# TensorE's filler matmuls in the first stage: 512 columns with a rest of 128, instead of 128 throughout

## The chip, the core and the metric

The kernel runs on one core of a Trainium2 chip. The metric is the device time of one execution in microseconds (us). The time of a kernel is the median of several executions.

## What is computed

Two layers in one program. The first is sliding-window attention with a linear bias by distance (8 batches, 8 heads, 576 positions, 64 numbers per head); the second is a feed-forward layer with a squared ReLU on the 4608 tokens that come out of it.

```python
scores = scale * np.matmul(q, k.transpose(0, 1, 3, 2))
bias = slopes[:, None, None] * (-np.abs(rel).astype(np.float32))[None, :, :]
mask = (rel >= 0) & (rel < window)            # window = 128
scores = np.where(mask, scores + bias[None], -1000000000.0)
attn = np.exp(scores - np.max(scores, axis=-1, keepdims=True))
attn = attn / (np.sum(attn, axis=-1, keepdims=True) + 1e-09)
attn_out = np.matmul(attn, v).astype(np.float32)
...
h = x @ w_in                                  # x: 4608 x 512, w_in: 512 x 2048
r = np.maximum(h, 0.0)
g = r * r
return (g @ w_out).astype(np.float32)         # w_out: 2048 x 512
```

## The kernel before

Attention works on blocks of 128 positions. For a block, q and k are loaded and cast to bf16, turned so that the head dimension lies on the partitions, multiplied into scores on TensorE, passed through the exponential on ScalarE, masked on VectorE (or given the bias by a matmul, for the first blocks), and multiplied with v ("pv", line 676). VectorE divides by the row sums (lines 693 and 702) and the result, turned again, is a slice of xT, the input of the feed-forward layer.

The feed-forward layer goes over nine groups of 512 tokens: 16 steps "up" (w_in against xT, lines 806 and 823), ReLU on ScalarE (line 770), square on VectorE (line 779), and 16 steps "down" (g against w_out, line 850) whose sums are copied to SBUF and stored. The groups of attention blocks and of the feed-forward layer are interleaved, so that TensorE has work of the second layer while the first waits.

The order of all instructions is fixed before anything is issued. Each piece of work is a `Task` with an estimated duration on each engine that could do it, its dependencies, and the PSUM banks or other buffers (`Slot`) that it takes and gives back. `Plan.order` runs through the estimated times, picks for each engine the next task by due time and a table of corrections (`ADJ`), and returns the list that is then issued. For a TensorE task that starts before 30 us of estimated time, it also notes `gap`, the time for which TensorE is expected to stand idle ahead of it while its PSUM bank is already free.

In the first stage the blocks come in one at a time and TensorE often waits. Two things are done about this. Right at the start, `warm_up` (line 483) issues eight matmuls of 512 columns on a zeroed tile `warm`. And the tasks that turn q and k ("tp", line 513), the scores, pv, the turning of x ("xp", line 722) and the up steps of the first groups ("unit", line 806) begin with `fill(task, slot)` (line 283): if the task's gap is over 200 ns, `FILL` (0.7) of it is filled with matmuls on `warm`, at 56 ns for each 128 columns. They write into the bank that the task itself is about to overwrite, so the task's own matmuls follow in the same bank. The fillers are issued after the order is fixed; the plan does not count them.

The first block (block 0) is loaded as float32 on SyncE's and ScalarE's queues and cast by VectorE (line 304, kq<-stage), first k, then q. Its transposes on TensorE come in two tasks: tp0.0 for k and tp0.1 for q; the results are copied out by VectorE (line 304, kqf<-tp) and ScalarE (line 306). The biases of the first scores are matmuls of 512 columns (line 624), the scores themselves line 633.

Of the kernel before, what the change touches and what calls it, by code (L numbers as in the profile page):

```python
# [27 lines left out]
FILL = 0.7  # L28
# [178 lines left out]
def kernel(  # L207
    ctx: ExitStack, tc: tile.TileContext, q, k, v, moe_w_in, moe_w_out, out
):
    nc = tc.nc  # L210
# [45 lines left out]
    warm = const.tile([128, 512], BF16)  # L256
# [24 lines left out]
        return slot  # L281

    def fill(task, slot):
        for _ in range(int(task.gap * FILL / 56.0) if task.gap > 200.0 else 0):
            nc.tensor.matmul(slot.tile[:, 0:128], warm[:, 0:128], warm[:, 0:128], start=True, stop=True)  # L285

    def tile_of(slot):
        return tiles[slot.tag][slot.idx]
# [179 lines left out]
    for what, key in at_first.items():  # L468
        n = int(what[1:])
# [22 lines left out]
    def transpose_kq(m, due):  # L492
# [12 lines left out]
        for i in range(2):  # L505
            st = Slot(TP if m else "o")

            def tp(i=i, st=st):
                fill(t_tp[i], bank_of(st, "tp"))
                st.tile = st.tile.bitcast(BF16)  # L510
                src = kq[s_kq[m].idx][:, i * d_model:(i + 1) * d_model]
                for j in range(C):
                    nc.tensor.transpose(st.tile[:, j * 128:(j + 1) * 128],  # L513
                                        src[:, j * 128:(j + 1) * 128], ident)
            t_tp[i] = plan.add({"PE": 4 * mm(128)}, due - 60 + i, tp,
                               [t_ident, t_tp[0] if i else last["tp"], t_kq[m][min(i, len(t_kq[m]) - 1)]],
                               [st] if i else [st, sT], [s_kq[m]] if i else [], name=f"tp{m}.{i}")

            pieces = [(0, C // 2), (C // 2, C)] if m < N_EV else [(0, C)]
            for c0, c1 in pieces:  # L520
                def evac(i=i, st=st, c0=c0, c1=c1, e=len(evs[i])):
                    o = tile_of(sT)[:, i * C + c0:i * C + c1, 0:n]
                    if split:
                        src = st.tile[:, 0:512].rearrange("p (i g c) -> p c g i", i=4, c=C)[:, c0:c1]
                        o = o.rearrange("p c (g i) -> p c g i", i=4)
                    else:
                        src = st.tile[:, 0:512].rearrange("p (c s) -> p c s", c=C)[:, c0:c1, 0:n]
                    copy(evs[i][e], o, src)
                w = (c1 - c0) * n
                evs[i].append(plan.add({"ACT": act(w), "DVE": dve_p(w, 1 if split else 2)}, due - 58, evac,  # L530
                                       [t_tp[i]], [], [st], name=f"ev{m}.{i}.{c0}"))
# [3 lines left out]
    def job(j, kind, ms, due):  # L535
# [24 lines left out]
        for z, grps in enumerate(bursts):  # L560
            def scores(grps=grps):
                for g2 in grps:
                    for r in range(2):
                        bank(sS[2 * g2 + r], f"s{r}")
                fill(t_s[grps[0]], sS[2 * grps[0]])
                for g2 in grps:
                    for jj in range(2):
                        c = 2 * g2 + jj
                        for c0, w, part, mk, mq in pieces:
                            for r in range(2):  # L570
                                rows = slice(64 * r, 64 * r + 64)
                                nc.tensor.matmul(sS[2 * g2 + r].tile[:, jj * 256 + c0:jj * 256 + c0 + w],  # L572
                                                 tile_of(s_kqT[mk])[rows, c, :], tile_of(s_kqT[mq])[rows, C + c, 0:w],
                                                 start=True, stop=True)
            deps = [last["s"]]
            for m in set(ms) | set(before.values()):
                deps += t_kqT[m]
            t = plan.add({"PE": 190.0 + len(grps) * 2 * len(pieces) * mm(128 if n == 128 else 64)}, due - 32, scores,
                         deps, sS[2 * grps[0]:2 * grps[-1] + 2], rel if grps[-1] else [],
                         name=f"s{ms[0]}" + (f".{z}" if len(bursts) > 1 else ""))  # L580
            last["s"] = t
            for g2 in grps:
                t_s[g2] = t
# [65 lines left out]
    def values(j, kind, i, m, nb, sP, t_P, mb, due):  # L649
# [14 lines left out]
        for hf in range(2):  # L664
            sv = Slot("h" if j < N_PVH else "a")

            def pv(hf=hf, sv=sv):
                fill(t_pvs[hf], bank_of(sv, "pv"))
                for hi in range(4):
                    h = 2 * hi + hf if kind == "lone" else 4 * hf + hi  # L670
                    for w, mk in parts:
                        if kind == "lone":
                            prob = lone_P(sP)[:, lone_place(h) * 128:(lone_place(h) + 1) * 128]
                        else:
                            prob = Pt[sP.idx][:, place(h)].rearrange("p t q -> p (t q)")[:, w]
                        nc.tensor.matmul(sv.tile[0:n, hi * (D + 1):(hi + 1) * (D + 1)], prob,  # L676
                                         tile_of(s_v[mk])[:, h, 0:D + 1], start=mk == parts[0][1], stop=mk == m)
# [240 lines left out]
```

The softmax here doesn't subtract the row's maximum and nothing guards it: scores larger than these inputs give would overflow.

## Time and profile before

| | |
|---|---|
| median of 4 runs | 313.43 us (313.13 to 313.82) |
| the profiled execution | 313.96 us |
| its span, first to last instruction | 312.2 us |
| TensorE busy | 306.7 us, 98% of the span |
| VectorE, ScalarE, GpSimd busy | 165.9, 169.4 and 106.2 us |
| filler matmuls (line 285) | 40, of 128 columns each, between 5.9 and 17.4 us |
| TensorE idle from 7.64 to 20.00 us | 12.36 - 11.28 = 1.08 us |
| TensorE idle from 20 to 100 us | 0 |

How to read it: the profile is one execution. A row of a view is an instruction or a merged run of like instructions, with its start from the beginning of the span, its duration, engine (PE is TensorE's matmuls, PEld its weight loads, DVE VectorE, ACT ScalarE), line, what it writes and reads, and in brackets the idle time before it and what ended that. Matmuls are pipelined, so the duration of one (0.22 us for 128 columns) is longer than the distance at which they start; the distance is what a matmul costs in a stream.

### The profile page before, as it was taken

The numbers are of one execution on the slowest core, as the hardware profiler recorded it, in microseconds if no ns is written. First come the engines' busy times: TensorE is split into PE (matmuls) and PEld (weight loads), VectorE is DVE, ScalarE is ACT, GpSimd is POOL, SyncE is SP. The second block draws the span as 40 slices with busy tenths as digits, with TensorE's granted clock in tenths as the row PEclk, the third lists the DMA queues.
The fourth block names the chain that finished last, engine by engine and source line by source line (L and its number), as shares of the span: only waits on it lengthen the run. The fifth ranks groups of instructions, "written<-read, shape, count | busy, mean of one in ns | idle before, by whom it ended". The sixth has DMA issues, their size and how long they took to land.

```text
span 312.2 us, 7098 instructions
## 1 busy us (share of the span) xinstructions
PE 306.7 (98%) x2792; PEld 175.0 (56%) x2792; DVE 165.9 (53%) x496; ACT 169.4 (54%) x324; POOL 106.2 (34%) x132
## 2 busy tenths in 40 slices
PE   8999999999999999999999999999999999999996
PEld 4579657676686744555455554555444444444443
DVE  5665457376667546878577665777222222222211
ACT  2586345496685545864597756664443443434400
POOL 8943586446640933613647364000000000000000
PEclk9999999999999999999999999999999999999999
DMA  9999999999999999998999999931111100011122
GB/s 130 160 206 206 174 195 173 167 164 161 164 162 166 148 166 198 134 133 163 160 170 179 162 157 178 191 78 53 53 34 44 57 36 34 36 36 34 34 86 84
DMA packets 166290, 39.54 MB, mean 127 GB/s; under 512 B 156400, under 2 KB 161776, under 8 KB 166256
## 3 DMA queue, kind: packets, MB, share of 16 engines
q0 software_dynamic: 115184, 18.10, 87.3%
q1 hardware_dynamic: 50640, 20.65, 37.5%
q8 instruction: 22, 0.36, 0.5%
q10 hardware_dynamic: 432, 0.33, 0.4%
q14 instruction: 12, 0.10, 0.1%
HBM read 36.70 MB, written 9.44 MB: 148 GB/s over the span
## 4 chain that ended last, share of the span: by engine, by line
PE 96%; DVE 1%; ACT 1%; issue 0%
PE o L850 40%; PE h L823 27%; PE h L806 14%; PE pv L676 6%; PE s L572 5%; PE wm L483 1%; PE tp L513 1%; DVE x L702 1%; PE tp L285 1%; PE xp L722 1%; PE s L624 0%; PE s L633 0%; ACT kqf L306 0%; ACT P L641 0%; DVE kqf L304 0%
## 5 line engine op out<-in xcount | busy, mean ns | idle before, releaser
L850 PE MATMUL o<-w_out_sb,g 128*128 128x512 bf16 (+2 forms) x592 | 141.8, 373 | 0.0
L770 ACT ACTIVATE rt<-h 128x512 bf16<-128x512 f32 (+1 forms) x145 | 86.1, 601 | 88.8 <-PE h L823 69.9
L779 DVE TENSOR_TENSOR g<-rt 128x512 bf16<-128x512 bf16 (+1 forms) x145 | 60.3, 419 | 95.5 <-ACT rt L770 95.0
L823 PE MATMUL h<-xT,w_in_sb 128*128 128x512 bf16 x384 | 96.7, 379 | 0.4 <-issue 0.4
L850 PEld LDWEIGHTS <-g 128*128 128x128 bf16 x592 | 54.2, 98 | 56.9
L596 ACT ACTIVATE P<-s 128x512 bf16<-128x512 f32 x120 | 62.2, 607 | 12.9 <-PE s L572 12.9
L823 PEld LDWEIGHTS <-w_in_sb 128*128 128x128 bf16 x384 | 35.4, 98 | 40.4 <-DMA xT<-x 0.5
L456 POOL DMA_DIRECT2D kq<-in_k_dram x39 | 33.4, 857 | 42.2 <-DMA kqT<-kq 34.0
L806 PE MATMUL h<-xT,w_in_sb 128*128 128x128 bf16 (+1 forms) x512 | 46.0, 246 | 0.0
L604 DVE TENSOR_TENSOR P<-P,masks 128x512 bf16<-128x512 bf16 x96 | 38.6, 418 | 11.6 <-ACT P L596 9.1
L806 PEld LDWEIGHTS <-w_in_sb 128*128 128x128 bf16 x512 | 39.0, 98 | 5.2
L461 POOL DMA_DIRECT2D vt<-in_v_dram x32 | 27.2, 851 | 33.2 <-PE pv L676 29.2
L456 POOL DMA_DIRECT2D kq<-in_q_dram x39 | 33.5, 860 | 7.8 <-PE h L806 2.1
L702 DVE TENSOR_TENSOR x<-pv,rec 128x256 bf16<-128x256 f32 (+1 forms) x80 | 32.0, 417 | 0.8
L676 PEld LDWEIGHTS <-P 128*128 128x128 bf16 (+1 forms) x576 | 24.2, 101 | 11.3 <-DVE g L779 1.3
L676 PE MATMUL pv<-vt,P 128*128 128x65 bf16 (+1 forms) x448 | 22.8, 194 | 0.0
L304 DVE COPY osb<-o 128x512 f32<-128x512 f32 (+1 forms) x19 | 13.0, 685 | 17.2 <-PE o L850 13.5
L306 ACT ACTIVATE osb<-o 128x512 f32<-128x512 f32 (+1 forms) x18 | 10.4, 580 | 21.5 <-PE o L850 21.5
L572 PEld LDWEIGHTS <-kqT 64*128 64x128 bf16 x448 | 12.4, 94 | 7.6 <-issue 7.6
L693 DVE RECIPROCAL rec<-pv 128x4 f32<-128x4 f32 (+1 forms) x80 | 12.4, 171 | 6.2 <-PE pv L676 5.4
L572 PE MATMUL s<-kqT 64*128 64x128 bf16 (+1 forms) x256 | 15.6, 210 | 0.0
L572 PE MATMUL s<-kqT,kqT 64*128 64x128 bf16 (+1 forms) x192 | 11.4, 210 | 0.0
(46 smaller groups left out, 105.1 us busy)
## 6 DMA issues: line engine op xcount, KB each, us to landing
out_dram<-osb SPq DMA_DIRECT2D x28, 256.0 KB, 5.5
kq<-in_k_dram POOLq DMA_DIRECT2D x31, 128.0 KB, 7.1
kq<-in_q_dram POOLq DMA_DIRECT2D x31, 128.0 KB, 7.7
vt<-in_v_dram POOLq DMA_DIRECT2D x24, 128.0 KB, 7.4
w_out_sb<-in_moe_w_out_dram POOLq DMA_DIRECT2D x4, 512.0 KB, 16.4
out_dram<-osb SPq DMA_DIRECT2D x14, 128.0 KB, 2.3
w_in_sb<-in_moe_w_in_dram POOLq DMA_DIRECT2D x3, 512.0 KB, 11.7
vf<-in_v_dram POOLq DMA_DIRECT2D x8, 128.0 KB, 7.1
```

The source lines that it names most:

```text
L456: nc.gpsimd.dma_start(view(kq[s_kq[m].idx], i), source(src, m, split))
L461: nc.gpsimd.dma_start(tile_of(s_v[m])[0:n, :, 0:D], source(v, m))
L572: nc.tensor.matmul(sS[2 * g2 + r].tile[:, jj * 256 + c0:jj * 256 + c0 + w], tile_of(s_kqT[mk])[rows, c, :], tile_of(s_kqT[mq])[rows, C + c ...
L596: nc.scalar.activation(flat(Pt[sP.idx]), sS[i].tile.rearrange("p (j t) -> p j t", j=2)[:, :, lo:hi], AF.Exp, bias=0.0, scale=scale)
L604: nc.vector.tensor_tensor(flat(Pt[sP.idx]), flat(Pt[sP.idx]), flat(masks), op=ALU.mult)
L676: nc.tensor.matmul(sv.tile[0:n, hi * (D + 1):(hi + 1) * (D + 1)], prob, tile_of(s_v[mk])[:, h, 0:D + 1], start=mk == parts[0][1], stop=mk ...
L702: nc.vector.tensor_tensor(o, heads(sv)[0:n, :, 0:D], sr.tile[0:n, :].unsqueeze(2).to_broadcast([n, 4, D]), op=ALU.mult)
L770: nc.scalar.activation(srt.tile[:, 0:n], slot.tile[:, 0:n], AF.Relu, bias=0.0, scale=1.0)
L779: nc.vector.tensor_tensor(o, i, i, op=ALU.mult)
L806: nc.tensor.matmul(slot.tile[:, f * w:(f + 1) * w], w_in_sb[:, cc, fc * 128:(fc + 1) * 128], xT[:, cc, lo:lo + w], start=cc == 0, stop=cc ...
L823: nc.tensor.matmul(slot.tile, w_in_sb[:, cc, fc * 128:(fc + 1) * 128], xT[:, cc, g * 512:(g + 1) * 512], start=cc == 0, stop=cc == C - 1)
L850: nc.tensor.matmul(slot.tile[:, 0:hi - lo], gt[:, fc, t * 128:(t + 1) * 128], w_out_sb[:, fc, lo:hi], start=fc == 0, stop=fc == FCB - 1)
```

## The change

The number of fillers n is worked out as before. They are then issued as n // 4 matmuls of 512 columns and n % 4 of 128 columns. The stationary operand (128 columns of `warm`) is the same, the moving operand and the written columns are four times as wide in the wide ones. Everything else is unchanged, the table of corrections too.

```diff
     def fill(task, slot):
-        for _ in range(int(task.gap * FILL / 56.0) if task.gap > 200.0 else 0):
-            nc.tensor.matmul(slot.tile[:, 0:128], warm[:, 0:128], warm[:, 0:128], start=True, stop=True)
+        n = int(task.gap * FILL / 56.0) if task.gap > 200.0 else 0
+        for w in [512] * (n // 4) + [128] * (n % 4):
+            nc.tensor.matmul(slot.tile[:, 0:w], warm[:, 0:128], warm[:, 0:w], start=True, stop=True)
```

## The prediction

> **What bounds the kernel now.** I read the page's busy table first, then the stretches of the first 20 us, then the fillers one by one, and last the chain of waits through them. The page:
>
> ```profile
> PE 306.7 (98%) x2792; PEld 175.0 (56%) x2792; DVE 165.9 (53%) x496; ACT 169.4 (54%) x324; POOL 106.2 (34%) x132
> ```
>
> TensorE is busy in 306.7 of 312.2 us. By stretch (columns: the stretch, then busy time and count of PE, of the weight loads, DVE, ACT and POOL, then granted clock, DMA share and GB/s):
>
> ```profile
> 5.86:7.64 1.78, 1.78 (x24) 1.78 (x23) 1.13 (x7) 0.23 (x1) 1.78 (x3) 1.00 1.54 155
> 7.64:20.00 12.36, 11.28 (x169) 8.21 (x167) 7.98 (x30) 8.81 (x26) 10.19 (x13) 1.00 1.92 177
> 20.00:100.00 80.00, 80.00 (x943) 57.28 (x940) 48.64 (x146) 49.84 (x97) 40.91 (x48) 1.00 1.89 175
> ```
>
> From 20 to 100 us TensorE never rests, so a delay or a gain of the first 20 us is carried to the end at full size. Only in those 20 us can fillers matter. These are all of them:
>
> ```profile
> L285 PE MATMUL tp<-warm x26: 219/219/314, 5.9 to 12.4; 128*128 128x128 bf16 x26
> L285 PE MATMUL xp<-warm x9: 219/219/229, 11.3 to 17.4; 128*128 128x128 bf16 x9
> L285 PE MATMUL pv<-warm x5: 219/219/219, 10.2 to 10.4; 128*128 128x128 bf16 x5
> ```
>
> That is 40 fillers. The timeline shows them in five groups, each just ahead of the task that asked for it: 22 at 5.86, 5 at 10.20, 4 at 11.26, 4 at 12.20 and 5 at 17.19. The chain of waits over 4 to 10 us tells which group is on the path:
>
> ```profile
> 4.79 0.43 PE tp L513 x4
> 5.21 0.85 PE s L624 x2
> 6.07 1.73 PE tp L285 x22
> 7.79 0.24 PE tp L513 x4
> 8.03 0.02 issue
> 8.05 0.44 DVE kqf L304
> 8.49 0.02 issue
> 8.51 0.39 ACT kqf L306
> ```
>
> The group of 22 is itself a link (1.73 us), followed by the transposes of block 0's q (line 513), their evacuation by DVE and ACT, and the first scores. What that group was to cover is DVE's cast of q, and the cast is done early:
>
> ```profile
> 6.00 0.89 DVE L304 CAST kq<-stage 128x512 bf16<-128x512 f32 x1 [0.33 <-DMA stage<-in_q_dram]
> ```
>
> It ends at 6.89, yet the first transpose starts at 7.63, behind the last filler. The fillers overrun their wait by about 0.7 us. The reason is in the spacing of the single rows: fillers start 0.107 us apart from 5.86 to 6.93, and 0.056 us apart from 7.07 on. The eight warm-up matmuls of 512 columns before them start 0.427 us apart, the 512-column matmuls of line 850 after 20 us 0.216 us apart. So TensorE runs at half speed until about 7.02 us and at full speed after it, though the granted-clock column reads 1.00 throughout; half the fill ran at the slow rate.
>
> **The change part by part.** No plan input changes: the fills are issued after the plan is made, no cost in it mentions them, so order, rings and DMA issues stay as they are. A group of n narrow fillers becomes n//4 of 512 columns and n%4 of 128, the same columns exactly: 22 gives 5 and 2, each 5 gives 1 and 1, each 4 gives 1. In sum 40 matmuls with 40 weight loads become 9 wide and 4 narrow with 13 loads; 27 of each go.
>
> *The group of 22.* At half speed, four narrow take 4 x 0.1067 = 0.427 and one wide takes 0.427: no difference. At full speed, four narrow take 4 x 0.0559 = 0.2236 (22 rows from 7.073 to 8.245, fillers and transposes alike) and one wide 0.2158 (line 850): 7.8 ns less. Before the switch 11 of the 22 have run, which is 2 wide ones and most of the third; the third ends then, two wide and two narrow follow at full speed. Only two wide ones save: about 16 ns. The transposes then start at 7.615 instead of 7.631. Their own wait, the cast, has long ended, so nothing takes this back, and the next on the chain, DVE's copy, follows them.
>
> *The five at 10.20.* The pv behind them starts 0.063 after the last filler where 0.056 is the spacing: it waits for ScalarE's exponentials (one ends at 10.430). 8 ns less filling becomes 8 ns more waiting: 0. *The four at 11.26*: they end at about 11.48, the transposes behind them wait until 11.649 for DVE's normalisation (ends 11.591): 0. *The four at 12.20*: the transposes start at once and would gain 8 ns, but end at 12.65 and their evacuation waits for DVE, which is busy until 13.05: 0. *The five at 17.19*: they end at 17.48 and the transposes wait until 17.858 for DVE: 0. If that cover were gone, each group would give 8 ns, 32 ns in all.
>
> *The 27 weight loads.* Matmuls of 128 columns run 0.056 apart with a load each, and the wide ones of line 850 also have one each; the loads lie beside the matmuls. 0. The trace shows no case where a load in this stage holds back a filler.
>
> *Waits.* A wide filler writes all 512 columns of its bank, a narrow one 128. Could it wait for a reader of the rest? Only the group at 12.20 waits at all, 0.221 after the row before it, and DVE's last reading of a pv bank ends at 12.138; it reads 256 columns in one instruction, so the narrow filler waits for all of it already. The others start on the spacing of the row before them or, at 17.19, on the 0.148 that also follows other score rows. Bounds: nothing below, 0.46 us above (the idle ahead of the transposes at 13.11, which would hide it). I take 0.
>
> Sum: 313.96 (the profiled execution; its span is 312.19 and 1.77 lies around it) - 0.016 = 313.94. The median of the four runs is 313.43, 0.53 below the profiled one; the same step gives **313.4 us**.
>
> What a page says against this: the Trainium skill, "TensorE: Matmul & The Clock Gate", section "Back-to-back issue gap", has a sustained spacing of about 81 ns for 128 columns and 131 ns for 512 in streams of load and matmul. By that estimate the first group would shrink by 20 x 81 - 5 x 131 = 965 ns and only the cast would stop it. This trace has 56 and 216 ns in just such streams, so the measurement decides. The same page, section "What's actually happening", says that the half-speed state ends after a busy window of about 3.4 us that runs freely, so that the switch falls elsewhere in each execution and does not depend on the matmuls' width. The trace has the switch once, 5.8 us after the first matmul, and can't show that it wanders.
>
> **The rivals.**
>
> *The fill gets shorter (faster).* If wide fillers ran closer than line 850's, or brought full speed earlier, the first transpose could move up until the cast stops it: 6.889 plus the 0.056 that a pv took to start after its exponential, 6.945. That is 7.631 - 6.945 = 0.69 at most: 313.43 - 0.69 = 312.7. All of it is needed to pass 0.2%. For it: the overrun is real and on the chain. Against: the warm-up's wide matmuls ran 0.427 apart, no better than four narrow ones. If full speed came with the first wide filler, the group would take 5 x 0.2158 + 2 x 0.0559 = 1.19 instead of 1.77, a gain of 0.58, just under 0.2%.
>
> *Full speed comes later (slower).* If the switch answers to something that narrow fillers have more of (they bring 22 matmuls and 22 loads where the new group has 7 and 7), it slips past the group. With all of it at half speed the 11 that ran fast cost 0.051 more each, 0.56; with the 4 transposes of block 0's q also slow, 0.20 more: 0.76, 314.2. If it slips behind the first scores and the next bias (two matmuls of 512, 0.21 more each), 0.4 more: 314.6. It decides the sign of the measurement if the switch comes after about 8.3 us instead of 7.02. For it: half of the execution's first fill hangs on this moment. Against: TensorE is without a gap from 1.19 to 8.3 in both kernels, with the same columns, and the switch came after a stretch that was mostly wide matmuls.
>
> *Nothing of note* is the forecast. That the change leaves the groups narrow is excluded by their counts, all of 4 or more.
>
> **How the numbers follow.** A measurement of this kernel can tell about 0.2%, 0.63 us, from no change: the four runs differ among themselves by 0.69. Nothing of note: 0.78. Shorter by the whole overrun: 0.10. Later full speed: 0.12. Hence faster 0.10, same 0.78, slower 0.12. The forecast's own range is the spread of the executions (313.13 to the profiled 313.96), 312.9 to 314.0 with a margin for a median of a few. The range reaches down to 312.8, to the edge of the faster case, and up to 314.2, the smaller price of the slower one.
>
> **What would show it.** In the profile after: line 285 has 9 matmuls of 128x512 and 4 of 128x128; the wide ones start 0.427 apart before the switch and 0.216 after it; the transposes of line 513 start at 7.6 if the switch is again near 7.0; the waits at 11.65, 13.11 and 17.86 stay. The first step is wrong if wide fillers are spaced otherwise, the slower rival is right if the switch sits behind the transposes in every execution, and the step on covered groups is wrong if a wait after 10 us moves by more than the group before it. The forecast is wrong if the time from the first filler to the first transpose differs by more than 0.6 us.

## The result, and the profile after

The changed kernel takes 314.73 us (median of 44 runs, 313.15 to 317.43), the kernel before 313.46 us (63 runs, 312.91 to 315.61): ratio 1.0035, 95% interval 1.0025 to 1.0045. That is 1.1 to 1.3 us slower, above the upper end of the forecast range (314.2). The two spreads overlap: under 314.0 us are 50 of 63 runs of the kernel before and 8 of 44 of the changed one. This share is used below beside the ratios, because it shows a loss that not every run has.

The profiled execution of the changed kernel took 315.65 us with a span of 313.9. From its page, TensorE's busy line and the line of the DMA queue that carries instructions (22 packets and 0.36 MB in the kernel before):

```profile
PE 306.5 (98%) x2765; PEld 173.4 (55%) x2765; DVE 165.8 (53%) x496; ACT 169.4 (54%) x324; POOL 106.3 (34%) x132
...
q8 instruction: 21, 0.34, 0.5%
```

TensorE does 0.2 us less work, and 27 pairs of load and matmul are gone. The stretches of the changed kernel, with the columns explained in the prediction:

```profile
5.86:7.64 1.78, 1.78 (x15) 1.03 (x14) 0.92 (x7) 0.24 (x1) 1.78 (x3) 1.00 1.68 155
7.64:20.00 12.36, 11.06 (x154) 7.41 (x151) 8.11 (x30) 8.96 (x27) 10.22 (x13) 1.00 1.92 177
20.00:100.00 80.00, 79.80 (x933) 56.95 (x930) 48.40 (x145) 49.48 (x97) 40.95 (x48) 1.00 1.83 172
100.00:200.00 100.00, 98.13 (x1003) 53.47 (x1000) 68.28 (x207) 62.07 (x117) 48.26 (x59) 1.00 1.76 163
```

Little of the new idle time lies in the first stage: from 7.64 to 20 us it grows from 1.08 to 1.30 us, from 20 to 100 us from 0 to 0.20. Between 100 and 200 us TensorE now rests for 1.87 us. The same stretch of the kernel before has 0.39:

```profile
100.00:200.00 100.00, 99.61 (x1016) 54.06 (x1014) 68.56 (x207) 62.76 (x119) 48.23 (x59) 1.00 1.87 166
```

It is one wait in one place. The chain of waits from 106 to 121 us, first of the changed kernel, then of the kernel before (start, length, what):

```profile
111.09 0.30 DVE osb L305
111.39 8.22 DMA xT<-x
119.61 0.30 issue
119.91 1.24 PE h L824 x5
```

```profile
117.57 0.24 PE pv L676 x8
117.81 0.39 issue
118.20 2.97 PE h L823 x13
```

The first 512-column up step (line 823, in the changed file 824) needs four slices of xT that DMA transposes write (landings, here and below, are read from the trace's records of semaphore updates). The fourth lands at 118.11 in the kernel before and at 119.82 in the changed one, and TensorE starts 0.09 us later in both. So the kernel before, too, waits for a DMA there, though the view puts its 0.39 us down to "issue". Up to this point the changed kernel is 0.22 us behind (at 20.6 us it waits for the first piece of w_out; before that it is 0.14 ahead); behind it, it is 1.71 behind to the end.

The DMA stream that feeds this point runs in a loop: GpSimd issues the loads of k and q into a ring of four buffers, SyncE issues the transposes out of them, and a buffer is loaded again only when its transpose has landed. The waits of GpSimd's queue (in total, times, longest), kernel before and changed:

```profile
POOL kq L456 <- DMA kqT<-kq: 34.0, 13, 6.0
```

```profile
POOL kq L457 <- DMA kqT<-kq: 40.8, 16, 6.0
```

GpSimd waits 6.8 us longer for transposes, though no load and no transpose was changed; part of this replaces other waits (those for pv fall from 29.2 to 26.6 us). Where the lag begins: the first of the loop's transposes lands at 57.79 instead of 57.47, the second at 62.28 instead of 60.74, and what SyncE issues lands 1.2 to 1.9 us late from there up to 79 us. Behind that the lag is not steady. GpSimd issues a load of q at 86.80 us, 0.23 earlier than in the kernel before, but it lands at 102.06, which is 2.39 later; the transpose that needs it goes out at 102.11 instead of 99.72, and SyncE issues the four transposes of xT behind it 1.3 to 1.7 us late. That the lag of 61 us is the one that arrives at 118 us is therefore argued, not shown.

What lies at 58 to 62 us is in the trace's records of DMA packets. Queue q8 has packets of 16,384 bytes, each about 1 us long, one for every 255 of TensorE's instructions (5605 rows, 22 packets): they bring TensorE's instructions. In the kernel before they start at 14.3, 23.8, 32.3, 43.3 and 56.8 us; in the changed one, within 50 of the same instruction numbers but with 54 instructions gone ahead of them, at 17.5, 26.9, 34.4, 45.9 and 58.9 us. The Trainium skill ("Runtime: NRT & Kernel Launch", section "Instruction fetch mechanics") states the same blocks, 256 instructions in 16 KiB, and calls the cost mostly hidden; for TensorE these traces agree (it rests 0 us from 20 to 100 us in the kernel before, over seven fetches), for the other users of the DMA engines they don't. One such fetch can be followed: in the changed kernel at 17.52 us, for 0.975 us. The sixteen DMA engines each end the first piece of w_out with a packet of 4 bytes. Fifteen of these come by 19.19 us, each 2.54 us after one of those of the piece before; the last comes at 20.46, 3.67 us after 16.79, and with it the whole piece lands at 20.75 us, 0.96 later than in the kernel before.

### The profile page after: what moved, and what is told of

Same layout as the page of the kernel before. It is cut to its first block, busy times and chain, and to the rows that moved or that the text cites. A ratio compares the mean times of both kernels' runs of the same rounds, so it can differ in the third digit from the quotient of the medians.

```text
span 313.9 us, 7044 instructions
## 1 busy us (share of the span) xinstructions
PE 306.5 (98%) x2765; PEld 173.4 (55%) x2765; DVE 165.8 (53%) x496; ACT 169.4 (54%) x324; POOL 106.3 (34%) x132
## 4 chain that ended last, share of the span: by engine, by line
PE 91%; DMA 4%; DVE 2%; POOL 1%; ACT 1%; issue 0%; POOLq 0%
PE o L851 38%; PE h L824 27%; PE h L807 13%; PE pv L677 6%; PE s L573 5%; DMA xT<-x 3%; DMA vf<-in_v_dram 2%; DVE x L703 1%; PE tp L514 1%; POOL kq L457 1%; PE xp L723 1%; ACT P L642 0%; DVE rec L694 0%; POOL w_in_sb L402 0%; ACT kqf L307 0%
## 5 line engine op out<-in xcount | busy, mean ns | idle before, releaser
L462 POOL DMA_DIRECT2D vt<-in_v_dram x32 | 27.1, 847 | 27.6 <-PE pv L677 26.6
L305 DVE COPY osb<-o 128x512 f32<-128x512 f32 (+1 forms) x19 | 13.0, 685 | 17.2 <-PE o L851 13.5
## 6 DMA issues: line engine op xcount, KB each, us to landing
w_out_sb<-in_moe_w_out_dram POOLq DMA_DIRECT2D x4, 512.0 KB, 17.2
```

Source lines behind the costliest of these rows:

```text
L462: nc.gpsimd.dma_start(tile_of(s_v[m])[0:n, :, 0:D], source(v, m))
```

## The experiments

The theory after these profiles, called FETCH: the wide fillers cost nothing, but 54 instructions fewer ahead of everything move TensorE's instruction fetches against the DMA traffic; a fetch in a bad place holds up one DMA engine for 1 us, the loop of loads and transposes carries the lag, and TensorE meets it at 118 us. The rival, WIDTH: the wide fillers themselves, or the altered timing of the first stage, cost it.

**The instruction count, with the widths kept.** The warm-up's eight matmuls of 512 columns can be cut into more matmuls with the same columns; at half speed that should cost no time.

```diff
-        for _ in range(N_WARM):
-            nc.tensor.matmul(s_warm.tile, warm[:, 0:128], warm, start=True, stop=True)
+        for w in [128] * 31 + [32] * 4:
+            nc.tensor.matmul(s_warm.tile[:, 0:w], warm[:, 0:128], warm[:, 0:w], start=True, stop=True)
```

Wide fillers, warm-up in 35 pieces:

> The changed kernel (wide fillers), with the eight warm-up matmuls of 512 columns cut into 31 of 128 and 4 of 32: the same 4096 columns, but 27 more pairs of load and matmul ahead of the fillers, so that everything behind the fillers has the instruction position on TensorE that it has in the kernel before. Theory FETCH (the loss comes from TensorE's 16 KB instruction fetches, which move by 54 instructions and so meet other transfers): the first fetch is back near 14.3 us, w_out's first piece lands near 19.8, and the time is that of the kernel before, ratio 1.000 within 0.001. Theory WIDTH (the wide fillers themselves or the earlier first stage cost it): ratio stays at 1.0035.

Measured: 313.43 us, ratio 0.9999 (0.9986 to 1.0013), 11 of 12 runs under 314.0; first fetch at 14.8 us. The loss is gone with every wide filler in place, and the wait at 118 us is what it was:

```profile
117.67 0.37 issue
118.04 2.97 PE h L824 x13
```

WIDTH falls here, but only if the cut warm-up is no cure of its own. One point of the expectation failed: w_out's first piece landed at 20.39, not near 19.8, and yet the time was good. So the early lag is not what costs.

Narrow fillers with the warm-up in 109 pieces (`[38] * 63 + [37] * 46`), and in 35 pieces:

> The kernel before (narrow fillers), with the warm-up's 4096 columns cut into 109 matmuls of 37 or 38 columns: 101 pairs or 202 instructions more, which with a fetch every 256 instructions is the same phase as 54 fewer. FETCH: fetches near 17.5 and 26.9 us as in the changed kernel, one more near 5 us, and the loss without any wide filler: ratio about 1.0035. WIDTH: ratio 1.000. If the short matmuls don't keep 31 ns at half speed, the fillers start later, which the trace shows.

> The kernel before with the same warm-up in 35 pieces: 54 instructions more ahead of the fillers. A control for the cut warm-up and a third position: the first fetch moves from 14.3 to about 11.8 us, where the loads are still limited by their issues and not by the DMA rings. FETCH: another time is allowed, my guess is no loss, ratio 0.998 to 1.001. WIDTH: 1.000.

Measured: 314.55 us with 109 pieces, ratio 1.0028 (1.0002 to 1.0054), 1 of 12 runs under 314.0; 313.65 us with 35, ratio 1.0003 (0.9989 to 1.0017), 9 of 12. The loss appears without a wide filler, and the first control is clean. The profiled execution of the 109-piece kernel is its fastest run (313.69) and has no wait at 118 us, so its trace shows the late transposes of 60 us but not the loss.

Narrow fillers, the four small groups left out (`for _ in range(n if n > 10 else 0)`):

> The kernel before without the 18 narrow fillers of the four small groups (they fill waits that remain; the group of 22 stays): 36 instructions fewer, no wide filler. FETCH: the first fetch moves to where the kernel before is at its instruction 279, about 15.9 us, two thirds of the way to 17.5; a loss of 0.001 to 0.0035 if the rings are already full there. WIDTH: ratio 1.000, since no filler is wide and those left out were covered.

Measured: 314.22 us, ratio 1.0012 (0.9995 to 1.0029), 3 of 12 under 314.0. The median says a loss, the interval doesn't; between the theories it is inconclusive. In its profiled execution, the slowest of its runs (316.1), TensorE waits 1.8 us at 118 us although the transpose at 61 us is only 0.13 late: the wait can also arise without that lag.

**Which fetch.** Pairs can also be added behind the first stage: pieces of the up steps of line 807 are multiplied in two halves. `skip` is 12 for the first run and 96 for a later one, n is 7 pieces (28 pairs) or 25 (100 pairs). The diff is shortened; `seen = [0]` stands ahead of it.

```diff
+                seen[0] += 1
+                cut = skip < seen[0] <= skip + n
+                for c0, c1 in [(0, w // 2), (w // 2, w)] if cut else [(0, w)]:
                     for cc in range(C):
-                    nc.tensor.matmul(slot.tile[:, f * w:(f + 1) * w], ..., xT[:, cc, lo:lo + w], ...)
+                        nc.tensor.matmul(slot.tile[:, f * w + c0:f * w + c1], ..., xT[:, cc, lo + c0:lo + c1], ...)
```

> The changed kernel, with 28 matmul pairs added behind the first stage: seven pieces of the up steps of group 0 after 22 us (from the thirteenth on) are multiplied in two halves of 64 columns. That costs about 2 ns a pair, 0.06 us. TensorE's first instruction fetch stays at 17.5 us as in the changed kernel, all later ones are back where the kernel before has them. Theory EARLY (the fetch at 17.5 us, when the first large weights fill the DMA rings, makes w_out's first piece land 1 us late, and that lag stays): ratio 1.0035. Theory LATE (the fetches after 25 us, above all those between 80 and 118 us, meet the transfers that x's transposes wait for): ratio 1.000.

Measured: 313.64 us, ratio 1.0011 (0.9995 to 1.0026), 8 of 12 under 314.0, and no wait of TensorE at 118 us in the profiled execution. The fetch at 17.2 us is still there, the loss is mostly not. The fetch shows in the packets too: of the sixteen closing packets of w_out's first piece, fifteen come 2.54 us after one of the piece before and one comes 3.65 us after it, but that one follows the earliest of all (15.41), and the piece lands at 19.63, on time. The 35-piece kernel had this piece late (20.39) without a loss. EARLY falls.

> The kernel with wide fillers and the warm-up in 35 pieces (first fetch near 14.5 us, ratio 0.9999), with 100 pairs added in the same place: 25 pieces of the up steps of group 0 in halves, about 0.2 us (0.0007) for themselves. 200 instructions more are 56 fewer in phase, so the fetches after 35 us stand where the changed kernel has them, and the first is as in the kernel before. EARLY: ratio 1.0007. LATE: 1.004.

Measured: 315.77 us, ratio 1.0065 (1.0043 to 1.0088). The added pairs cost what was estimated: the halves start 0.029 us apart where whole pieces start at 0.056. But behind them TensorE stands still, in a row of the timeline that waits for nothing the profile shows:

```profile
32.33 1.44 PE L812 MATMUL h<-xT,w_in_sb 128*128 128x128 bf16 x23 [0.89 <-issue]
```

From there on the kernel is 1.05 us further behind. A fetch starts at 29.9 us, and the halves use instructions up almost twice as fast; that TensorE ran out of them is likely, but argued. Of the 2.3 us over the 35-piece kernel, 1.3 go to the pairs and this stall. The 1 us left agrees with LATE in size, but the profiled execution (314.67, among the faster ones) doesn't have it: its fetch near 59 us starts at 60.1, the transpose of 61 us is on time, and TensorE doesn't wait at 118 us. The run is inconclusive.

> The changed kernel with 28 pairs added at 84 to 87 us: seven pieces of group 2's up steps in two halves of 128 columns, 0.06 to 0.3 us of cost for themselves. The fetches up to 82 us stay where the changed kernel has them, those after 87 us are back where the kernel before has them. If the fetches just ahead of the wait at 118 us (93, 104 and 117 us) make the loss: ratio 1.000 to 1.001. If those between 25 and 82 us do: 1.0035 to 1.0045.

Measured: 314.65 us, ratio 1.0038 (1.0018 to 1.0058), 1 of 12 under 314.0. The fetches after 87 us are back in place and the loss stays; what matters lies between 26 and 82 us. The waits of TensorE in its profile:

```profile
PE h L829 <- DMA xT<-x: 2.0, 1, 2.0
```

**More positions, and the controls.** Wide and narrow fillers with the warm-up in 136 pieces (128 pairs more, a whole fetch), and wide ones with 62:

> Wide fillers with the warm-up's 4096 columns in 136 matmuls of 30 or 31 columns: 128 pairs more than the changed kernel, 256 instructions, one fetch more ahead of the first stage and all others in the places of the changed kernel. FETCH (the position of TensorE's instruction fetches sets the time): the loss that the 35-piece warm-up took away is back, ratio 1.003 to 1.0035. WIDTH, or a theory in which a finer warm-up as such cures the loss: 1.000, as with 35 pieces.

> Narrow fillers with the same 136-piece warm-up: 256 instructions more than the kernel before, the fetches in its places and one more ahead. It is the control for the 109-piece run. FETCH: ratio 1.000. If the very fine warm-up (or the additional early fetch) caused the loss of the 109-piece run: 1.0028 here too.

> Wide fillers with the warm-up in 62 pieces of 66 or 68 columns: 54 pairs more than the changed kernel, 54 instructions more than the kernel before, the position of the narrow kernel with the 35-piece warm-up, which gave 1.0003. FETCH: ratio 1.000 within 0.001 though the fillers are wide.

Measured: wide with 136 pieces 314.89 us, ratio 1.0048 (1.0030 to 1.0065), none of 7 under 314.0. Wide with 62: 313.56, ratio 1.0002 (0.9990 to 1.0014), 9 of 12. Both as FETCH has it: the same wide fillers lose or don't lose by the count ahead of them. The narrow control with 136 pieces missed: 313.82, ratio 1.0023 (1.0004 to 1.0042), 7 of 12. Its profiled execution (315.59) is one of its slower ones: the fetch is at 57.8 us instead of 56.8, the transpose of 61 us is 1.08 late, and TensorE waits 1.5 us at 118 us. Whether a very fine warm-up costs something of its own or the fetch sits on an edge there is open, and the 109-piece run is no clean proof that narrow fillers alone can lose. The profile of the wide 136-piece kernel has the wait again:

```profile
PE h L824 <- DMA xT<-x: 1.8, 1, 1.8
```

**The fetches from 56 us on, and a clean narrow case.** `skip` is 64 for the first; the second is the kernel before with `range(13 if n > 10 else 0)`.

> The changed kernel with 28 pairs added at 50 to 55 us: seven pieces of group 1's up steps in two halves of 128 columns, about 0.07 us for themselves. The fetches at 17.5, 26.9, 34.4 and 45.9 us stay where the changed kernel has them; the one at 58.9 goes back to about 56.6, and later ones to where the kernel before has them. If the fetch at 58.9, in the middle of the DMA transposes of 58 to 63 us, starts the lag: ratio 1.000 to 1.001, and the transposes that land at 60.7 and 62 us in the kernel before are on time within 0.6. If one of the four earlier fetches does: 1.0035.

> The kernel before with 13 fillers of 128 columns, all in the first group, and none in the small groups: 27 pairs fewer than the kernel before, the instruction positions of the changed kernel with its warm-up and without any wide filler. FETCH: fetches near 17.5 and 58.9 us, the transposes late from 61 us on, ratio 1.002 to 1.0035. WIDTH: ratio 1.000, or a little less, since the first group overruns its wait less.

Measured: with the pairs at 50 us 313.69, ratio 1.0002 (0.9985 to 1.0019), 8 of 12 under 314.0; the fetch is at 56.9, and the transposes that land at 60.74 and 65.24 us in the kernel before are 0.28 and 0.08 late (the 62 us of the expectation is a landing of the changed kernel). The fetches at 71.7 and 81.6 us go back with it, to 70.7 and 78.7, so this run alone doesn't say which of the three matters. The 13 narrow fillers: 314.81, ratio 1.0051 (1.0023 to 1.0079), 1 of 9, fetch at 58.5, the transpose late by 1.21. Narrow fillers with the original warm-up lose too when 27 pairs are missing. That its transposes of q start at 6.96, 0.67 earlier than in the kernel before, brought nothing. The profiled execution is its second fastest run (314.01): there the next transpose is only 0.04 late and the xT slice landed at 118.14.

All positions together. "Fetch" is the start of the fetch nearest to 58 us and "late" how much later than 60.74 us the transpose lands that lands then in the kernel before, both from one profiled execution each:

```
kernel                    fillers  fetch  late   ratio   under 314.0
before                    narrow   56.8   0.00   1       50 of 63
35-piece warm-up          wide     57.3   0.76   0.9999  11 of 12
62-piece warm-up          wide     52.8   0.66   1.0002   9 of 12
28 pairs at 50 us         wide     56.9   0.28   1.0002   8 of 12
35-piece warm-up          narrow   51.9   0.46   1.0003   9 of 12
28 pairs at 22 us         wide     56.5  -0.06   1.0011   8 of 12
22 fillers only           narrow   56.9   0.13   1.0012   3 of 12
136-piece warm-up         narrow   57.8   1.08   1.0023   7 of 12
109-piece warm-up         narrow   59.2   1.99   1.0028   1 of 12
changed                   wide     58.9   1.53   1.0035   8 of 44
28 pairs at 84 us         wide     58.6   2.05   1.0038   1 of 12
136-piece warm-up         wide     58.5   1.33   1.0048   0 of 7
13 fillers only           narrow   58.5   1.21   1.0051   1 of 9
35 pieces, 100 pairs more wide     60.1  -0.01   1.0065   0 of 9
```

Fetches at 58.5 to 59.2 us lose and those up to 57.3 don't, at either width; the one at 57.8 lies between, and the run with 22 fillers only is a doubtful case without this lag. The run with 100 pairs more can't be placed, since its pairs and its stall alone put it above 314.0; but its fetch at 60.1 us, with transposes still under way, delayed none of them in its profile.

The two fetches behind this one move with it: they start at 71.2 to 71.9 and at 80.5 to 82.4 us in the five kernels with the fetch at 58.5 to 59.2, by 70.7 and 78.7 at the latest in the kernels without a loss, and at 71.2 to 71.3 and 79.0 to 79.8 in the two doubtful ones (136 pieces narrow, 22 fillers only). They separate the kernels as well as the first does, and no run moves one of the three alone. For the first speaks that the transposes are late from 61 us on, ahead of the other two. What is special there shows in the stretches around it, kernel before and changed (the last two columns are the DMA share, the packets' time over that of 16 engines, which is above 1 where packets overlap, and GB/s):

```profile
55.00:58.00 3.00, 3.00 (x24) 2.11 (x22) 0.57 (x3) 1.34 (x3) 0.00 (x0) 1.00 2.38 155
58.00:63.00 5.00, 5.00 (x49) 3.30 (x47) 2.12 (x5) 2.10 (x4) 4.35 (x5) 1.00 1.44 173
63.00:66.00 3.00, 3.00 (x31) 2.22 (x26) 1.72 (x5) 2.67 (x6) 1.13 (x3) 1.00 3.11 137
```

```profile
55.00:58.00 3.00, 3.00 (x23) 2.02 (x21) 0.68 (x2) 1.49 (x3) 0.00 (x0) 1.00 2.26 138
58.00:63.00 5.00, 5.00 (x43) 3.27 (x43) 2.01 (x5) 1.96 (x5) 2.82 (x4) 1.00 1.71 155
63.00:66.00 3.00, 3.00 (x37) 2.24 (x32) 1.72 (x5) 2.67 (x6) 2.44 (x3) 1.00 1.79 124
```

Before 58 us the queues are deep (2.38), and by the packet records most of it is loads. From 58 to 63 us it is mainly transposes, 1.44, and GpSimd issues its next loads only as they land: 4.35 us of issuing in this stretch in the kernel before, 2.82 in the changed one, whose transposes end later; the next burst of loads (3.11 in the last row) comes after 65 us instead of at 63. The fetch at 56.8 lies in the deep part, the one at 58.9 in the transposes. All sixteen DMA engines end the second transpose within 0.2 us of one another in both kernels (60.54 to 60.74 and 62.08 to 62.28 us), where in the load of w_out one engine alone was late. That it is this lock-step of the transposes that makes the second place dear is argued from these rows; no run tried it by itself, and the fetch at 60.1 us in the run with 100 pairs speaks against every such place being dear.

**The place where the loss is paid.** The stores of groups 0 to 2 left out, in the changed kernel and in the kernel before:

```diff
-            for r, p, n in rows:
+            for r, p, n in rows if g > 2 else []:
```

> The changed kernel without the stores of groups 0 to 2 (the first 1536 rows of the output aren't written), 3 MB less on the DMA rings before 118 us. If the loss is realised where TensorE waits for the DMA transposes of x near 118 us, less traffic brings them in time and the loss goes: the ratio to the kernel before falls to that of the next run, the same edit on the kernel before, within 0.001. If the loss is TensorE's own, the two stay 0.0035 apart.

> The kernel before without the stores of groups 0 to 2. The wait of 0.4 us near 118 us goes, ratio 0.998 to 0.999. It is the base for the run above.

Measured: 314.16 and 314.07 us, ratios 1.0023 (1.0011 to 1.0035) and 1.0018 (1.0007 to 1.0029). With less DMA traffic ahead of 118 us the xT slices land at 110.96 and 110.62, TensorE waits for none of them, and the difference of the two widths is down to 0.0005. This agrees with the loss being paid there. It doesn't prove it, because leaving the stores out also moves the fetch of the kernel before, from 56.8 to 58.4 us, beside the other's 58.6. The second expectation failed: both got slower, not faster. In the profile of the kernel before without these stores, the wait of 0.4 us is gone and TensorE ends 0.42 us earlier; but in both profiles the end of the span comes 3.9 and 3.8 us after the last weight load of the down steps starts, in the kernel before 3.1: the last store takes 2.1 and 2.0 us to land instead of 1.6. Why is open.

## Why the prediction was wrong

*"The 27 weight loads ... 0"* is the step that failed, with its sister *"order, rings and DMA issues stay as they are"*. I priced an instruction only by what it does on its engine. Each also takes its place in the instruction stream, and 54 fewer move every later fetch, up to 118 us by 1.2 to 4.4 us, against the DMA traffic. The runs put that at 1.1 to 1.3 us in the typical run; with the count restored by a finer warm-up it is nothing (0.9999, 0.9986 to 1.0013), and with the same count missing and no wide filler the loss is there (1.0051). That the count ahead decides, and not the width, is shown; which of the fetches at 59, 72 and 82 us carries the loss, and by what path it reaches 118 us, is argued.

*"A delay or a gain of the first 20 us is carried to the end at full size"* failed too. I took TensorE's unbroken work from 20 to 100 us for the bound and didn't look at the stretch behind it, whose wait for xT decides: what happens ahead of 118 us counts only as far as it outlasts that wait. Of the 0.37 us by which the transposes of q start earlier in the changed kernel, 0.14 are left at the first pv already, which waits 0.2 us for the load of v. Nine of the other profiled kernels start the transposes of block 0's q at 6.95 or 6.96 instead of 7.63 us, and none is faster than the kernel before.

*The group of 22* was priced rightly: wide fillers started 0.216 us apart at full speed in every trace, and the one whole distance at half speed, in the 35-piece kernel, is the predicted 0.427 (the 0.420 of the changed kernel is that of a filler during which the speed changed). But the switch came at 6.3 us in the changed kernel's profile, not 7.0, and before the fillers in most others: it wanders from execution to execution, which the one trace of the kernel before couldn't show. Hence the start at 7.26:

```profile
5.86 1.56 PE L286 MATMUL tp<-warm 128*128 128x512 bf16 x7
7.26 0.83 PE L514 MATMUL tp<-ident,kq 128*128 128x128 bf16 x12
```

The floor that I gave for it, 6.945 by the cast, was met in those nine kernels; in the 109-piece one, whose cast ends at 6.36 instead of 6.89, the start is 6.80.

*The covered groups* and *the waits* were right: the waits ahead of 11.65, 13.11 and 17.86 are all there, each 0.14 earlier as the whole stage is.

*The rivals.* The slower one had the right sign and a near price (314.2 to 314.6), but its mechanism, a later full speed, is not what happened: the switch came earlier. A rival in which removed instructions cost time was missing.

## What to carry to other kernels

A removed or added instruction also shifts the fetches of all that follow, and these share the DMA engines with the kernel's data (one fetch made an engine 1.1 us late in the load of w_out). Before a change that only alters an instruction count is called free, it pays to find the places where a DMA is on the edge of being late (here a wait of 0.39 us put down to "issue") and which fetches move into the transfers ahead of it. And a comparison of two kernels of different instruction counts should be made once more with the count evened out: here cutting the warm-up into 35 or 62 smaller matmuls did it at no cost that the runs show (0.9999 to 1.0003).

## What the runs showed of the hardware

- TensorE's instructions come in packets of 16,384 bytes, one for every 255 or so of its instructions, each 0.9 to 1.4 us long on one DMA engine where a data packet of 1,024 bytes took 0.098. The same transpose landed at 60.74 us in the kernel before, with a fetch at 56.8, and at 62.28 in the changed one, with the fetch at 58.9. In the load of w_out, a fetch at 17.52 us (changed kernel) and one at 17.24 (28 pairs at 22 us) each made one of sixteen engines 1.1 us late; the load as a whole was late in the first case, where that engine was the last (16.79), and not in the second, where it was the first (15.41).
- TensorE's switch to full speed wanders between executions: it fell at 7.0 us in the kernel before and ahead of 5.74 us in the same kernel without the stores, at 6.3 us in the changed kernel and ahead of 5.7 us in its runs with pairs at 22, 50 and 84 us. Up to the earlier switch the matmuls are the same in each of these pairings.
- At half speed, matmuls of 37 or 38 columns, each with a weight load of 128 columns, mostly started 0.030 to 0.033 us apart; at full speed, halves of 64 columns start 0.029 apart where whole ones of 128 start at 0.056. A hundred such pairs in a row were followed by a stop of TensorE of 1 us (0.89 in the row above, by its matmuls' modelled ends) that no shown wait explains.
